# Weights for a gated feed-forward: nine transfers with the cast on GpSimd's queue instead of staged loads and casts on ScalarE, with the order of all steps made anew

## The chip, the cores and the metric

The kernel runs on one core of a Trainium2 chip. The metric is the device time of the core in microseconds. Before the change the median of four runs is 265.79 us (265.08 to 266.65).

## The reference

Two stages follow each other. The first is a linear recurrence with a complex decay per channel; its output is the `x` of the second, a feed-forward with a sigmoid gate. Shapes: batch 4, 8 heads, 768 positions, 48 channels per head; 3072 tokens of 384, inner width 1536. All inputs and the output are float32.

```python
mag = np.sqrt(a_re * a_re + a_im * a_im)
scale = np.minimum(mag, 0.999) / (mag + 1e-06)
a_re_n, a_im_n = (a_re * scale, a_im * scale)
for t in range(S):
    new_re = ar * S_re - ai * S_im
    new_im = ar * S_im + ai * S_re
    kv = np.einsum('bhd,bhe->bhde', k[:, :, t], v[:, :, t])
    S_re, S_im = (new_re + kv, new_im)
    y[:, :, t] = np.einsum('bhd,bhde->bhe', q[:, :, t], S_re)
...
gate = 1.0 / (1.0 + np.exp(-(x @ w_gate)))
val = x @ w_val
return (gate * val @ w_out).astype(np.float32)
```

## The kernel before

The positions are cut into six chunks of 128, which makes 24 slabs (a batch and a chunk; a slab is 128 positions by 384 channels). Slabs are taken in seven groups of 4, 4, 4, 4, 4, 2 and 2 (`SIZES`); a group is one chunk of two or four batches.

For each slab the decay is brought into logarithmic and angular form. `lr` and `la` load the real and imaginary part of `a` (L568), `sq` squares them on ScalarE, for slabs 4 to 8 on VectorE (L595, L598), `add` and `min` form and cap the squared magnitude, `lnm`, `lna` and `inv` are Ln, Ln and Exp on ScalarE over a whole group (L619 to L630), `r` divides the imaginary by the real part, and `atan` is the arctangent on ScalarE over a whole group (L714). `add`, `min`, `r` and `qke` run on VectorE for group 0 and on GpSimd from group 1 on. TensorE sums logarithms and angles along the positions by multiplying with triangular matrices (`cl` L645, `ct` L728 or L750). From `cl` come the growth factors `ee` (Exp, L652 and L654); from `ct`, after taking off whole turns (`r16` on VectorE, `nid` on TensorE L764) and `ab` (VectorE, L785), come sine and cosine, `cs` (L796 to L799). `cr` (ScalarE, L774) keeps the last angle of a chunk for the next one; from chunk 2 on `hop` (L741), a small accumulating DMA from GpSimd's queue, adds it.

`lk`, `lq` and `lv` load k, q and v (L568). `v16` (GpSimd, L700) turns v into float16, `qke` multiplies q and k by `ee`, and `ks` and `qs` by `cs` (VectorE, L809). Then comes attention within the chunk: transposes `tp` (TensorE) copied by `qkT` (VectorE), or a transposing DMA from slab 13 on (L830), scores `sc` (L866), masked by `mst` (VectorE), output `y` (L932, L934) together with the state carried on by `kv`, `P`, `u` and `x16`. `y16`, `xp` and `xt` put the result into transposed float16 form; `xt` of all slabs of a group is the moving operand of the feed-forward.

For each group and each of 12 blocks of 128 inner channels, `pg` and `pv` are three matmuls each with `wg16` and `wv16` (L971), `tanh` on ScalarE makes the gate (L981), and `p` on VectorE multiplies gate and value (L987). `po` multiplies with `wo16` (L1007, three parts of four blocks), `ot` copies out of PSUM and `st` stores.

The weights are kept in SBUF as float16 for the whole run. They arrive in nine parts of 768 KB of float32: `wg` and `wv` for three thirds of the inner width, `wo` for three groups of four blocks. Each part is loaded on SP's queue into a staging buffer (`lw`, L540) and cast from there by ScalarE (`wg`, `wv`, `wo`, L547). The staging buffers are those of `p`: tag `"p"`, two of them, each holding two parts (`t_stage`, L465). A block's matmul waits for the cast of its part: `pg` and `pv` of blocks 0 to 3, 4 to 7 and 8 to 11 need part 0, 1 and 2, and `po`'s parts 0, 1 and 2 need `wo` 0, 1 and 2.

The order is written out. Every step has a due time in the table `TIMES`; `Plan.order` sorts all steps by it, and each engine executes its own steps in that order, SP and GpSimd their DMAs among them. `SLOTS` lists which buffer each tile takes, and where table sets of ScalarE change, a table load is put in (L1035). `WARM` gives, for some steps, a number of dummy matmuls of a zero matrix that TensorE does just ahead of the step (L1041), 212 in all. The semaphores of SP's DMAs are eight; each DMA there waits for the one eight places earlier.

```python
t_p = kind("p", 2, [L, NFB, NT], F16)
t_stage = kind("p", 2, [L, 2, DFF], F32)
...
for _ in range(WARM.get(key, 0)):
    nc.tensor.matmul(warm_of(tiles[st[2][0]]), zero, zero, start=True,
                     stop=True)
st[0](tiles)
```

Of the kernel before, what the change touches and what calls it, by code (L numbers as in the profile page):

```python
# [9 lines left out]
FT = mybir.ActivationFunctionType  # L10
# [26 lines left out]
    "lw": [  # L37
        19.49, 20.04, 30.47, 40.31, 47.2, 47.61, 46.25, 73.886, 81.267],
    "wg": [
        24.732, 43.572, 53.59],  # L40
    "wv": [
        28.793, 45.685, 56.737],
    "wo": [
        52.038, 79.752, 85.177],
    "lr": [
        0.6, 1.01, 3.72, 5.64, 7.56, 10.44, 19.08, 14.28, 24.164, 37.02,
        37.98, 45.84, 63.086, 73.476, 67.716, 68.676, 92.809, 95.026, 97.906,
        95.986, 131.5, 133.365, 166.445, 167.265],
    "la": [
        2.76, 4.68, 6.6, 1.42, 8.52, 13.32, 21.96, 12.36, 32.97, 42.78, 32.01,  # L50
        38.94, 66.756, 70.596, 69.636, 65.796, 93.556, 93.966, 98.866, 99.826,
        132.955, 137.236, 169.565, 166.855],
    "sq": [
        6.25, 8.17, 10.09, 9.13, 12.01, 16.953, 29.367, 20.803, 42.465,
        50.194, 44.948, 50.931, 71.7, 79.015, 73.917, 74.654, 98.023, 100.439,
        105.897, 105.16, 146.848, 141.69, 174.014, 172.8],
    "add": [
        7.119, 9.039, 10.959, 9.999, 13.027, 17.97, 30.384, 21.82, 44.139,
        51.099, 47.431, 55.186, 72.902, 81.822, 75.617, 78.122, 98.928,
        101.957, 109.068, 112.251, 148.29, 150.03, 174.919, 177.613],  # L60
    "min": [
        10.465, 11.539, 19.034, 31.449, 54.283, 59.633, 83.264, 79.763,
        104.673, 116.121, 154.388, 178.678],
    "lna": [
        10.958, 34.367, 63.259, 83.639, 112.029, 159.027, 181.383],
    "lnm": [
        12.335, 32.99, 64.636, 86.554, 117.088, 158.29, 180.646],
    "inv": [
        13.712, 35.875, 68.63, 87.931, 114.146, 159.895, 186.735],
    "r": [  # L70
        16.087, 15.221, 37.42, 40.36, 73.856, 70.175, 90.609, 100.197,
        124.829, 119.361, 164.309, 187.64],
    "cl": [
        13.863, 17.228, 15.601, 18.161, 37.278, 38.144, 35.069, 39.237,
        79.005, 71.394, 66.186, 69.454, 88.548, 112.467, 99.081, 114.653,
        139.626, 135.097, 135.743, 129.837, 162.384, 180.788, 181.657, 184.024],
    "ee": [
        15.356, 20.061, 21.541, 20.801, 38.125, 38.991, 37.252, 40.084, 82.9,
        73.177, 72.437, 70.483, 89.395, 116.263, 113.406, 115.523, 140.473,
        139.564, 137.607, 138.347, 163.231, 182.12, 182.86, 185.995],  # L80
    "scr": [
        28.52, 21.41, 22.37, 30.88, 42.23, 57.44, 48.02, 41.27, 83.456,
        82.777, 82.087, 83.736, 106.956, 116.819, 117.379, 117.099, 146.14,
        145.3, 145.86, 145.58, 176.685, 190.661, 183.416, 188.831],
    "rbe": [
        57.99, 60.708, 90.82, 119.819, 149.384, 194.771, 197.005],
    "lk": [
        15.24, 9.48, 27.12, 11.4, 21, 29.1, 48.3, 52.98, 74.436, 64.836,
        81.677, 86.967, 100.786, 106.546, 105.586, 123.678, 118.069, 107.506,
        158.098, 136.09, 168.605, 171.775, 175.235, 181.208],  # L90
    "lq": [
        16.2, 17.16, 30.06, 18.12, 41.82, 36.06, 48.78, 57.03, 75.396, 72.516,
        82.367, 96.946, 101.746, 109.426, 108.466, 126.359, 133.775, 112.315,
        159.058, 138.46, 172.445, 190.251, 175.905, 189.111],
    "lv": [
        28.11, 31.16, 40.86, 39.9, 62.676, 71.556, 63.846, 56.07, 84.016,
        103.666, 122.761, 102.706, 111.535, 144.89, 85.648, 118.479, 156.968,
        104.626, 156.558, 117.659, 135.13, 146.42, 181.619, 188.421],
    "v16": [
        39.783, 42.121, 46.855, 43.39, 68.913, 77.059, 81.246, 63.163, 92.946,  # L100
        113.205, 126.59, 121.702, 117.024, 153.811, 92.37, 144.793, 180.823,
        110.823, 176.251, 132.347, 152.257, 166.285, 198.483, 214.257],
    "qke": [
        19.69, 23.984, 34.227, 21.687, 52.522, 45.094, 57.64, 60.536, 84.746,
        87.087, 88.848, 102.912, 106.442, 117.6, 132.924, 129.129, 145.949,
        140.486, 162.548, 143.032, 182.185, 195.134, 183.946, 193.373],
    "atan": [
        17.39, 42.195, 77.638, 108.405, 128.051, 188.766, 189.503],
    "ct": [
        19.7, 21.064, 23.315, 22.491, 43.722, 45.48, 51.057, 48.16, 90.342,  # L110
        83.489, 86.435, 91.96, 122.348, 115.95, 130.651, 127.476, 140.92,
        146.098, 165.596, 164.583, 194.132, 197.143, 197.956, 204.107],
    "r16": [
        22.553, 23.019, 24.85, 23.518, 45.882, 46.973, 52.55, 56.052, 91.189,
        86.013, 87.282, 99.842, 124.156, 117.252, 131.498, 128.52, 146.898,
        149.406, 166.443, 165.446, 194.979, 199.289, 201.811, 206.04],
    "nid": [
        23.153, 23.961, 25.45, 24.124, 46.996, 47.573, 53.15, 57.25, 91.798,
        90.988, 90.012, 102.317, 125.791, 119.412, 132.144, 129.507, 150.204,
        155.105, 169.642, 166.242, 195.995, 201.192, 203.297, 213.571],  # L120
    "cr": [
        27.266, 30.169, 31.326, 28.423, 49.037, 51.668, 68.26, 59.378, 92.586,
        93.433, 97.177, 102.68, 127.311, 127.681, 144.386, 131.028, 156.626,
        160.632, 170.32, 167.763],
    "cs": [
        23.575, 26.109, 30.54, 27.636, 49.407, 48.039, 58.591, 59.748, 94.28,
        91.429, 95.543, 103.527, 126.154, 119.776, 133.911, 129.871, 151.782,
        155.469, 171.166, 166.606, 196.359, 201.556, 203.661, 214.248],
    "ks": [
        25.316, 27.635, 35.691, 32.495, 55.006, 49.236, 60.355, 66.904,  # L130
        96.644, 92.718, 98.376, 106.137, 127.627, 121.248, 135.716, 136.582,
        154.275, 159.937, 172.965, 169.831, 198.423, 202.845, 207.249, 215.537],
    "qs": [
        26.182, 28.501, 37.157, 33.361, 56.518, 50.702, 63.908, 69.383, 97.51,
        94.278, 104.374, 109.857, 132.43, 122.58, 138.513, 139.379, 156.452,
        167.841, 177.88, 174.431, 199.755, 211.988, 209.18, 218.223],
    "ab": [
        30.233, 27.169, 48.77, 48.039, 57.872, 58.938, 92.161],
    "tp": [
        27.788, 31.585, 30.692, 29.501, 38.79, 41.199, 40.553, 41.646, 62.391,  # L140
        60.202, 61.296, 63.485, 74.229, 75.522, 74.675, 72.911, 106.813,
        111.37, 98.634, 102.479, 116.596, 107.91, 113.113, 118.966, 154.258,
        143.708],
    "qkT": [
# [127 lines left out]
        203.866, 211.451, 220.798],  # L272
    "xq": [
        126.769, 141.65, 140.4, 164.125, 173.985, 179.589, 185.921, 200.886,
        213.009, 210.201, 219.548],
}
SLOTS = {
    "a2": "0101010",
# [793 lines left out]
```

## Time and profile before

| what | value |
|---|---|
| median of four runs | 265.79 us |
| profiled execution, its own time | 265.76 us |
| its span, first to last instruction | 263.9 us |
| TensorE matmuls busy | 244.2 us (93%), 2128 instructions |
| weight loads into TensorE | 155.4 us (59%) |
| VectorE | 210.4 us (80%), 363 |
| ScalarE | 190.2 us (72%), 297 |
| GpSimd | 144.4 us (55%), 156 |
| SP's DMA queue (q1) | 41.28 MB in 174320 packets, 76.5% of 16 DMA engines |
| GpSimd's DMA queue (q0) | 0.03 MB in 512 packets, 0.2% |
| mean granted TensorE clock | 0.974 |

The span is the stretch from the first to the last instruction; the execution's own time has 1.8 us more around it. In the page, PE, ACT, DVE, POOL and SP are TensorE, ScalarE, VectorE, GpSimd and SyncE; L568 and the like are lines of the kernel. A slice row gives the busy tenths of 40 equal slices of the span. A table of windows gives, for each stretch, its length and then the busy time and the number of instructions (x) of TensorE's matmuls, its weight loads, VectorE, ScalarE and GpSimd, then the granted clock, the DMA engines' busy share and GB/s. The chain of waits is followed back from the last instruction (here, from the last in a window): each piece has its start, its length, and the engine or transfer that held the end up.

### The profile page before, as it was taken

Reading aid. Unit: us, or ns where it says so; the run is one execution under the profiler, and the core shown is the slowest. Engines: PE = TensorE matmul, PEld = TensorE weight load, DVE = VectorE, ACT = ScalarE, POOL = GpSimd, SP = SyncE. Lnnn points to the kernel's source line nnn. Section 1 sums busy time; section 2 is a strip of 40 time slices with the busy share of each in tenths; the row PEclk is TensorE's granted clock in tenths of the full one; section 3 lists DMA queues with packets and bytes.
Section 4 is the critical chain, followed back from the end, with each engine's and each line's share of the span. In section 5 each row is a group of like instructions: output and inputs, shape, how many; then the busy total and the mean of one; then the engine's idle time right before and its main releaser. Section 6 shows DMA issues by size and latency. Waiting matters only on the chain.

```text
span 263.9 us, 5745 instructions
## 1 busy us (share of the span) xinstructions
PE 244.2 (93%) x2128; PEld 155.4 (59%) x2128; DVE 210.4 (80%) x363; ACT 190.2 (72%) x297; POOL 144.4 (55%) x156
## 2 busy tenths in 40 slices
PE   8188399989899999999999999999999999999995
PEld 8145287454457664556775456754567554678784
DVE  2648997887999669898998869989957979796662
ACT  1899999689999899799669956778792674115140
POOL 3031207667499997789978399831989604011000
PEclk9959779999999999999999999999999999999999
DMA  7999999899999579995787987869986276540101
GB/s 150 211 192 292 224 222 191 207 362 138 123 195 248 161 152 163 218 190 122 95 190 161 199 192 73 160 132 210 216 156 114 31 149 79 112 132 30 45 18 62
DMA packets 174860, 41.68 MB, mean 158 GB/s; under 512 B 167768, under 2 KB 172528, under 8 KB 174832
## 3 DMA queue, kind: packets, MB, share of 16 engines
q1 hardware_dynamic: 174320, 41.28, 76.5%
q8 instruction: 17, 0.28, 0.4%
q0 software_dynamic: 512, 0.03, 0.2%
q14 instruction: 11, 0.09, 0.1%
HBM read 30.74 MB, written 4.76 MB: 135 GB/s over the span
## 4 chain that ended last, share of the span: by engine, by line
PE 61%; ACT 15%; SPq 8%; DMA 7%; DVE 4%; issue 4%; POOL 1%; ACTq 0%; DVEq 0%
PE o L1007 16%; PE v L971 14%; PE g L971 13%; SPq L568 7%; PE ct L750 4%; PE cl L645 4%; DMA stage<-in_moe_w_gate_dram 3%; PE sc L866 3%; ACT L1035 3%; DMA stage<-in_moe_w_val_dram 2%; ACT g L981 2%; PE y L934 2%; DMA a<-in_a_im_dram 1%; PE y L932 1%; ACT sq L598 1%
## 5 line engine op out<-in xcount | busy, mean ns | idle before, releaser
L981 ACT ACTIVATE g<-g 128x512 f16<-128x512 f32 (+1 forms) x84 | 43.3, 539 | 35.6 <-PE g L971 28.5
L987 DVE SCALAR_TENSOR_TENSOR p<-g,v 128x512 f16<-128x512 f16 (+1 forms) x84 | 49.3, 606 | 14.2 <-PE v L971 6.9
L971 PE MATMUL v<-xt,wv 128*128 128x512 f16 (+1 forms) x252 | 56.6, 348 | 0.9 <-ACT g L981 0.9
L971 PE MATMUL g<-xt,wg 128*128 128x512 f16 (+1 forms) x252 | 56.8, 348 | 0.0
L1007 PE MATMUL o<-wo,p 128*128 128x384 f16 (+1 forms) x300 | 54.6, 319 | 0.0
L707 POOL TENSOR_TENSOR qk<-qk,ee 128x768 f32<-128x768 f32 x20 | 39.7, 2055 | 8.5 <-ACT ee L654 4.6
L604 POOL TENSOR_TENSOR lm<-sq 128x384 f32<-128x384 f32 x20 | 21.9, 1097 | 39.8 <-DVE sq L595 24.2
L874 DVE TENSOR_TENSOR mst<-sc,msk_t 128x512 f16<-128x512 f32 x48 | 32.2, 685 | 5.8 <-PE sc L866 5.2
L971 PEld LDWEIGHTS <-wg 128*128 128x128 f16 x252 | 24.0, 98 | 20.9 <-issue 2.7
L971 PEld LDWEIGHTS <-wv 128*128 128x128 f16 x252 | 23.8, 98 | 20.1 <-issue 2.0
L1007 PEld LDWEIGHTS <-p 128*128 128x128 f16 x300 | 27.1, 97 | 13.8 <-issue 0.7
L1035 ACT ACT_TABLE_LOAD x23 | 29.5, 1283 | 0.4
L645 PE MATMUL cl<-lm,wl_t 128*128 128x384 f32 x48 | 22.6, 560 | 7.0 <-ACT lm L625 6.3
L809 DVE TENSOR_TENSOR kst<-qk,cs 128x768 f16<-128x768 f32 x24 | 25.1, 1047 | 1.5 <-issue 0.8
L809 DVE TENSOR_TENSOR qst<-qk,cs 128x768 f16<-128x768 f32 x24 | 24.7, 1032 | 0.0
L636 POOL TENSOR_TENSOR a<-a 128x768 f32<-128x768 f32 x10 | 19.0, 1902 | 7.6 <-ACT a L630 7.5
L854 DVE COPY qkT<-tp 128x1024 f16<-128x1024 f16 x26 | 17.5, 683 | 4.3 <-PE tp L848 4.3
L1041 PEld LDWEIGHTS <-zero 128*128 128x128 f16 x212 | 16.3, 114 | 6.4 <-issue 4.6
L598 ACT ACTIVATE sq<-a 128x768 f32<-128x768 f32 x19 | 15.7, 851 | 5.7 <-DMA a<-in_a_im_dram 5.6
L847 PE MATMUL tp<-idn_t,kst 128*128 128x128 f16 x104 | 15.4, 231 | 4.6 <-DVE cs L785 2.5
L796 ACT ACTIVATE cs<-ct 128x384 f32<-128x384 f32 x17 | 8.3, 490 | 15.5 <-PE ct L764 15.4
L700 POOL TENSOR_SCALAR v<-v 128x384 f16<-128x384 f32 x24 | 14.5, 604 | 5.3 <-DMA v<-in_v_dram 1.8
(76 smaller groups left out, 455.4 us busy)
## 6 DMA issues: line engine op xcount, KB each, us to landing
a<-in_a_re_dram SPq DMA_DIRECT2D x24, 192.0 KB
a<-in_a_im_dram SPq DMA_DIRECT2D x24, 192.0 KB
qk<-in_k_dram SPq DMA_DIRECT2D x24, 192.0 KB
qk<-in_q_dram SPq DMA_DIRECT2D x24, 192.0 KB
v<-in_v_dram SPq DMA_DIRECT2D x24, 192.0 KB
out_dram<-ot SPq DMA_DIRECT2D x23, 192.0 KB
stage<-in_moe_w_gate_dram SPq DMA_DIRECT2D x3, 768.0 KB
stage<-in_moe_w_val_dram SPq DMA_DIRECT2D x3, 768.0 KB
```

The source lines that it names most:

```text
L568: nc.sync.dma_start(heads(dst), src[b, :, c * L:(c + 1) * L].rearrange("h t d -> t h d"))
L604: eng(g).tensor_tensor(out=T[LM][:, s], in0=T[SQ][:, 0], in1=T[SQ][:, 1], op=ALU.add)
L636: eng(g).tensor_tensor(out=T[A][:, 1, i:j], in0=T[A][:, 1, i:j], in1=T[A][:, 0, i:j], op=ALU.mult)
L645: nc.tensor.matmul(T[CL][:, :HD], wl_t, T[LM][:, s], start=True, stop=True)
L707: eng(g).tensor_tensor(out=T[QK], in0=T[QK], in1=T[EE], op=ALU.mult)
L809: nc.vector.tensor_tensor(out=T[SL][i].rearrange("p h (r x) -> p h r x", r=2)[:, :, :, 0:D], in0=heads(T[QK][:, i]).unsqueeze(2) .broadcas ...
L874: nc.vector.tensor_tensor(out=T[MS], in0=T[SC], in1=msk_t.unsqueeze(1).broadcast_to([L, 4, L]), op=ALU.mult)
L971: nc.tensor.matmul(T[ACC][:, :nt], w[:, j, fb * 128:fb * 128 + 128], T[XT][:, j, :nt], start=(j == 0), stop=(j == 2))
L981: nc.scalar.activation(out=T[G16][:, :nt], in_=T[PG][:, :nt], func=FT.Tanh, scale=0.5)
L987: nc.vector.scalar_tensor_tensor(out=T[PT][:, fb, :nt], in0=T[G16][:, :nt], scalar=1.0, op0=ALU.add, in1=T[PV][:, :nt], op1=ALU.mult)
L1007: nc.tensor.matmul(T[PO][:, :wd], T[PT][:, fb, s * L:(s + 1) * L], wo16[:, fb, c0:c0 + wd], start=(fb == 0), stop=(fb == NFB - 1))
L1035: nc.scalar.preload_act_table_set(SETS[key[1]])
```

## The change

The nine parts of the weights no longer pass through staging buffers. Each is one DMA on GpSimd's queue that reads float32 from HBM and writes float16 straight into `wg16`, `wv16` or `wo16`. The steps `lw` on SP and the casts on ScalarE are gone, and so is the second use of the `p` buffers. The tables `TIMES`, `SLOTS` and `WARM` are all new: steps come in another order on every engine, tiles take other buffers, and the dummy matmuls are 150 instead of 212, put in other places. What each step computes is unchanged.

```diff
@@ tiles @@
     t_p = kind("p", 2, [L, NFB, NT], F16)
-    t_stage = kind("p", 2, [L, 2, DFF], F32)
@@ weights @@
-    def stage(n, i, key, dst, src):
-        ST = f"stage_{n}"
-        if not i:
-            t_stage(ST)
-
-        def e(T):
-            nc.sync.dma_start(
-                T[ST][:, i].rearrange("p (j f) -> p j f", j=dst.shape[1]), src)
-
-        load = add(("lw", 2 * n + i), e, after=[("lw", 2 * n)] if i else [],
-                   new=[] if i else [ST], use=[ST] if i else [])
-
-        def e(T):
-            nc.scalar.activation(
-                out=dst, in_=T[ST][:, i].rearrange("p (j f) -> p j f",
-                                                   j=dst.shape[1]),
-                func=FT.Copy)
-
-        return add(key, e, after=[load], use=[ST])
-
     gv_keys, ou_keys = [], []
-    for n, f in enumerate(range(0, DFF, 512)):
-        for i, (nm, dst, src) in enumerate((("wg", wg16, moe_w_gate),
-                                            ("wv", wv16, moe_w_val))):
-            gv_keys.append(stage(
-                n, i, (nm, n), dst[:, :, f:f + 512],
-                src[:, f:f + 512].rearrange("(j p) f -> p j f", p=128)))
-    for n, j in enumerate(range(0, NFB, 4)):
-        ou_keys.append(stage(
-            3 + n // 2, n % 2, ("wo", n), wo16[:, j:j + 4],
-            moe_w_out[j * 128:(j + 4) * 128].rearrange("(j p) f -> p j f",
-                                                       p=128)))
+    for i, f in enumerate(range(0, DFF, 512)):
+        for nm, dst, src in (("wg", wg16, moe_w_gate), ("wv", wv16, moe_w_val)):
+            def e(T, dst=dst, src=src, f=f):
+                nc.gpsimd.dma_start(
+                    dst[:, :, f:f + 512],
+                    src[:, f:f + 512].rearrange("(j p) f -> p j f", p=128))
+
+            gv_keys.append(add((nm, i), e))
+    for i, j in enumerate(range(0, NFB, 4)):
+        def e(T, j=j):
+            nc.gpsimd.dma_start(
+                wo16[:, j:j + 4],
+                moe_w_out[j * 128:(j + 4) * 128].rearrange(
+                    "(j p) f -> p j f", p=128))
+
+        ou_keys.append(add(("wo", i), e))
@@ dummy matmuls @@
 WARM = {
-    ('cl', 0): 78,
-    ('cl', 1): 3,
-    ('cl', 2): 4,
+    ('cl', 0): 41,
+    ('cl', 2): 8,
     ('cl', 3): 2,
-    ('ct', 0): 16,
-    ('ct', 1): 2,
-    ('ct', 3): 14,
-    ('sc', 0, 0): 15,
-    ('sc', 1, 0): 8,
-    ('sc', 1, 1): 8,
-    ('sc', 2, 1): 12,
-    ('sc', 3, 0): 9,
-    ('y', 3): 5,
-    ('pg', 0, 0): 8,
-    ('pg', 0, 10): 3,
-    ('cl', 6): 15,
-    ('ct', 4): 8,
-    ('cl', 10): 2,
+    ('ct', 0): 7,
+    ('ct', 2): 16,
+    ('y', 2): 11,
+    ('sc', 3, 1): 9,
+    ('pg', 0, 0): 11,
+    ('cl', 4): 15,
+    ('cl', 6): 30,
 }
```

Of the new order, the stretch in front of the first feed-forward block, as each engine has it (numbers are slabs, for `lnm`, `lna`, `inv`, `atan` groups, for weights parts):

```
ScalarE: cs0 cs1 cr0 cr1 cr3 cs3 cr2 cs2 lnm1 lna1 ee6 inv1 ee4 ee5 ee7 atan1 sq9 cs5 cr4 cr5 cs4 sq11 sq10 lna2 cs7 cr7 tanh
VectorE: ks0 qs0 sq6 ks1 r16.2 ab3 qs1 ab2 ks3 qke2 ... mst3 ks5 y16.3 xt0 qs5 y16.2 xt3 r16.7 ks4 xt2 xt1
GpSimd:  add4 add5 add7 v16.0 min4 wg0 add6 min6 r6 r4 wv0 v16.1 add8 add9 qke4 wg2 qke5 v16.3 wv2 v16.2 add10 wg1 min8 qke6 wv1 add11 v16.6 min10 qke7 add12 wo1 v16.4 arr1 r8 wo0 r10 ... wo2
```

In the order before, ScalarE has in this stretch the casts wg0 behind cs0, wv0 behind cr3, wg1 behind atan1, wv1 behind sq10, wo0 and wg2 behind cr5, and wv2 behind the first tanh; wo1 and wo2 come later, behind sq13 and lna3.

## The prediction

> **What bounds the kernel now.** I read the page's slices first, then the busy time by stages, then the chain of waits for the first 64 us, then the rows of the lines that the change touches. In the first fence come slices of 6.6 us, in the second stages with each engine's busy us and instruction count.
>
> ```profile
> PE   8188399989899999999999999999999999999995
> ACT  1899999689999899799669956778792674115140
> DMA  7999999899999579995787987869986276540101
> ```
>
> ```profile
> 0.00:60.00 60.00, 45.72 (x408) 31.89 (x408) 44.29 (x81) 49.04 (x63) 22.71 (x33) 0.89 0.97 228
> 60.00:70.00 10.00, 8.75 (x72) 4.83 (x70) 8.43 (x12) 9.89 (x15) 6.93 (x7) 1.00 0.92 111
> 70.00:80.00 10.00, 9.81 (x72) 5.41 (x71) 9.59 (x14) 9.90 (x16) 7.59 (x8) 1.00 0.95 186
> 80.00:100.00 20.00, 19.51 (x199) 12.63 (x198) 15.32 (x30) 19.22 (x24) 18.98 (x20) 1.00 0.78 178
> 100.00:120.00 20.00, 19.72 (x140) 10.70 (x139) 18.54 (x27) 18.21 (x31) 15.76 (x15) 1.00 1.10 197
> 120.00:240.00 120.00, 119.82 (x1042) 72.92 (x1040) 101.70 (x173) 77.61 (x136) 72.44 (x78) 1.00 0.73 139
> ```
>
> There are two regimes. From 70 us to 240 TensorE stands still for 0.19 + 0.49 + 0.28 + 0.18 = 1.14 us, so the end is set by how early the dense stretch of matmuls begins and by the few gaps after that. Before 60 us TensorE is the least loaded of the resources that matter: its 45.7 busy us contain nearly all of the dummy matmuls (17.9 us for the kernel), while ScalarE and the DMA engines (share 0.97) are full. The change can only pay before about 60 us and in the gaps just behind.
>
> The chain of waits (start, us, what) shows how the dense stretch begins:
>
> ```profile
> 33.66 4.02 SPq L568
> ...
> 43.09 6.39 DMA stage<-in_moe_w_val_dram
> ...
> 49.50 1.49 ACT wv L547
> ...
> 51.01 7.59 DMA stage<-in_moe_w_gate_dram
> ...
> 58.62 1.48 ACT wg L547
> ...
> 60.12 1.28 ACT L1035
> ...
> 61.41 0.60 ACT g L981
> ```
>
> The weights arrive late on SP's queue, ScalarE casts them in order, and the first tanh (L981, 61.41) stands behind the casts of 56.50 and 58.62. The timeline of TensorE has the first gate matmul at 59.17, with the blocks behind it broken by waits for that tanh (0.64 us at 63.9).
>
> ```profile
> L547 ACT ACTIVATE wg<-stage x3: 1467/1483/1483, 26.0 to 58.6; 128x1536 f16<-128x1536 f32 x3
> L547 ACT ACTIVATE wv<-stage x3: 1476/1484/1485, 30.6 to 61.9; 128x1536 f16<-128x1536 f32 x3
> L547 ACT ACTIVATE wo<-stage x3: 1467/1484/1484, 56.5 to 92.3; 128x1536 f16<-128x1536 f32 x3
> ...
>   DMA stage<-in_moe_w_val_dram: 1.0, 1
>   DMA stage<-in_moe_w_out_dram: 0.9, 2
>   DMA stage<-in_moe_w_gate_dram: 0.8, 2
> ```
>
> ```profile
> L741 POOL DMA_DIRECT2D a<-cr x16: 793/819/1282, 85.8 to 206.4; - x16
> ```
>
> The first of these two fences has min/median/max ns of the casts and how long ScalarE sat idle before them; the second is the only DMA that GpSimd issues in this trace.
>
> **What the Trainium skill says.** "DMA: Bandwidth & Descriptors", section "Anatomy of one DMA — SWDGE (gpsimd) path": a DMA from GpSimd has its descriptors written by GpSimd's own cores; many can be written "before the incremental cost shows up"; its fit is 2.0 us plus bytes at 436 GB/s, an estimate of 3.8 us for 786 KB. The hops agree as to the fixed part (1.9 to 4.8 us to landing); no large one is in the trace. The same page, "Queues, rings and completion order": each DMA engine takes turns between queues by packets. So a weight on GpSimd's queue should not wait behind SP's backlog; this trace has no two loaded queues to show it. "SBUF — State Buffer", "SBUF: two separate sides": a VectorE instruction in a two-port mode locks GpSimd out of writing descriptors, 620 ns becoming about 3100. "VectorE: DVE Perf Modes", "Mode 2×_2P": that mode needs its single source in SBUF. From 43 to 60 us VectorE's one-source work here reads PSUM (r16, ab, y16, qkT, xt, P) and the rest has two inputs, so I expect no such lock there; the hops among similar work (median 819 ns) agree.
>
> **The change, part by part.**
>
> *Casts.* 9 x 1.48 = 13.3 us leave ScalarE, seven of them (10.4 us) starting by 61.9, with three waits for weights of 2.7 us in all. They can't all be gained: VectorE is 44.3 busy of 60, and 9.28 + 9.38 of 20 between 20 and 40.
>
> *Path to the first gate matmul.* I walk the new order with durations of the trace; a start-to-start distance is used where the trace has it. Up to the first cs (24.50) ScalarE's steps are the same kinds in the same sequence. Then: cs, cs at 1.28 and three cr at 0.50 to 28.6; the third cs waits for VectorE's ab, which stands behind ks 0.86, qs 0.87, sq 0.87, ks 0.86, r16 0.47, ab 0.47 from 25.8, thus 30.2; cs 0.93, cr 0.50, cs 0.93, table 1.28 lead to Ln at 33.9 (before 35.32); Ln 1.39, Ln 1.49, ee 0.75, Exp 1.50 to 39.05. The two r on GpSimd (1.90, 1.82) end at 42.8, and group 1's arctangent starts at 42.9, against 44.92 before.
>
> *GpSimd's queue.* Behind the r stand, in this order: weight wv0, v16, add, add, qke, wg2, qke, v16 of slab 3, wv2, v16 of slab 2. That last one feeds y of slab 2 and so the first gate matmul. Three weight issues are on this path. Take q for one: nothing in the trace has 384 rows. Below, the hop's 0.82 + 0.07 gap = 0.89; above, the lock's 3.1. I take 1.0, since it writes more descriptors, but without a lock. Sum from 42.8: 3 x 1.0 + v16 3 x 0.58 + add 2 x 1.05 + qke 2 x 1.90 = 10.6, so v16 of slab 2 ends at 53.4. VectorE's queue from there: y16 0.48, xt 0.30, r16 0.47, ks 0.86, two xt 0.60, with y itself 0.35: 3.1, so the first gate matmul at 56.6. That is 2.6 before 59.17. The walk leaves out waits that I can't see (landings of q, k and v, pipeline gaps), so I book 1.6 of it: about 57.6.
>
> *DMA.* A weight at the 304 GB/s of the window 50 to 60 costs 2.6 us of all engines. Before, seven weights are issued by 51.5, and SP, which reuses eight semaphores, stood still for 4.02, 3.40 and 3.71 us in its issues (33.7, 53.2, 56.7). Afterwards six stand before the first tanhs and wo follows in GpSimd's queue later; nine issues of 0.35 to 1.04 us leave SP, so the a, q, k and v loads behind them go sooner. I book no separate gain; it is what lets the walk hold. A weight lands, by the trace's 6.4 and 7.6 us, in time: wv2 issued by 52.8 is there by 60.4, and its first use comes about four blocks of 0.65 us after the first, roughly 60.5, so a wait of up to 0.5 is possible; wg1 (issued about 55) and wv1 (about 59) are needed nine and more blocks in.
>
> *Behind the first matmul.* TensorE's gaps are 1.25 us from 60 to 70 and the 1.14 above. In that time casts at 61.9, 86.2 and 92.3 (4.4 us) leave a ScalarE that is 99% busy to 80 and 96% to 100. GpSimd takes four issues more there, being 18.98 busy of 20 from 80 to 100, but these come before 80. I book 0.8 of 2.4.
>
> *Dummies, buffers, order.* Dummies fall from 212 to 150; they fill idle time, so nothing is gained. They hold the granted clock at 1.00 from 36 us; should a window of some 6.8 us drop to half, as at 29.4 here, up to 3 us are lost. Freed p buffers and the order after 100 us: nothing, TensorE is full there and its work is the same.
>
> Sum: 1.6 + 0.8 = 2.4. The profiled execution took 265.76, its span being 263.9 and 1.8 lying around it, and stands 0.03 below the median of 265.79: 263.4.
>
> **Rivals.**
>
> *GpSimd's issues are dear (slower).* A weight's issue holds GpSimd for q, and three stand ahead of slab 2's v16. For it: 384 rows on either side against the hop's 16, and the skill's lock. Against it: the hops, and VectorE's sources in PSUM. Each 0.1 costs 0.3 us; it decides from q = 1.0 + 2.4/3 = 1.8, where the gain is gone, and makes the kernel measurably slower from 2.25. At q = 2.6 the time is 263.4 + 3 x 1.6 = 268.2.
>
> *VectorE and the DMA engines take ScalarE's place (no change).* VectorE has under 5 us of slack between 20 and 60 and the DMA share is 0.97; the transfer with a cast may hold the engines longer. Then the first gate matmul comes at about 58.8 and the gaps remain: 265.4. Against it: the walk went through VectorE's queue and still gained.
>
> *All of it is gained (much faster).* The walk's whole 2.6 and 2.0 of the gaps: 261.2. For it: ScalarE is on the chain in nearly every step from 8.5 to 26 and again from 49.5; against: no walk of this kind is without waits.
>
> *The change does what it says* without a rival: the plain loads and casts are gone from SP's and ScalarE's order, and nine DMAs stand in GpSimd's.
>
> **How the numbers follow.** Forecast 0.42 (its own range 262.3 to 264.4), all gained 0.15, no change 0.21, dear issues 0.17, another cause of loss (clock, late weight) 0.05. About 0.5%, 1.3 us, is what a measurement can tell from no change, so faster is below 264.5 and slower above 267.1. Faster 0.57, same 0.22, slower 0.21. Leaving a tenth on each side: 261.2 to 267.8.
>
> **What would show it.** Right: first gate matmul between 56.5 and 58.2, arctangent of group 1 near 43, no wait for a weight over 0.5 us, GpSimd's DMA rows near 1.0 us, TensorE's gaps from 60 to 120 below 2 us. Wrong: DMA rows of GpSimd above 1.8 us, slab 2's v16 later than 55, a gate or value matmul released by a weight's landing, or a clock below 1.00 after 40 us.

## The result, and the profile after

The median after is 264.8 us (264.25 to 266.14, 41 runs), before 265.75 us (264.47 to 267.29, 62 runs); the ratio is 0.9965, 95% interval 0.9955 to 0.9976. So 0.95 us (0.35%) are gained of the 2.4 us forecast, within the 0.5% that the prediction took for what a measurement can tell from no change. A second measurement, on another occasion, gave 0.9938 (0.9919 to 0.9957): after took 264.76 us again, before 266.56. So the size of the gain depends on how before runs on that occasion. The forecast of 263.4 us is missed; the time lies inside the range of 261.2 to 267.8 us. A few runs lie more than 1.5% above the fastest of their kernel; ratios leave them out, medians hold them. The span is 263.1 us (263.9 before), the mean granted clock 0.974 in both.

The slices of after, each 6.6 us:

```profile
PE   6086778999999999999999999999999999999995
ACT  3699599299999578999459648758974373214240
DMA  7999999999699959975699969869964455551011
```

The busy us and instruction counts by stages, in the columns used for before:

```profile
0.00:60.00 60.00, 42.52 (x351) 27.81 (x352) 45.49 (x83) 44.60 (x62) 29.12 (x38) 0.89 1.02 183
60.00:70.00 10.00, 10.00 (x75) 5.80 (x74) 8.84 (x12) 9.73 (x15) 6.78 (x8) 1.00 0.90 128
70.00:80.00 10.00, 9.99 (x71) 5.31 (x69) 8.79 (x14) 9.95 (x19) 9.79 (x11) 1.00 1.22 210
80.00:100.00 20.00, 19.49 (x204) 12.60 (x203) 16.63 (x30) 14.36 (x18) 19.15 (x22) 1.00 0.87 164
100.00:120.00 20.00, 19.52 (x128) 10.55 (x127) 18.16 (x26) 19.44 (x33) 16.07 (x16) 1.00 0.89 159
120.00:240.00 120.00, 119.34 (x1075) 72.56 (x1074) 103.39 (x176) 73.92 (x130) 69.47 (x75) 1.00 0.72 137
```

From 60 to 80 us TensorE's gaps are closed: 1.25 and 0.18 us more busy than before. Behind that TensorE stands still a little more than in before: 0.02, 0.20 and 0.48 us in the last three stages.

The weights' rows on GpSimd (busy us, mean ns of one):

```profile
L526 POOL DMA_DIRECT2D wg<-in_moe_w_gate_dram x3 | 2.7, 895 | 0.1
L526 POOL DMA_DIRECT2D wv<-in_moe_w_val_dram x3 | 2.5, 840 | 0.1
L533 POOL DMA_DIRECT2D wo<-in_moe_w_out_dram x3 | 2.5, 820 | 0.0
```

An issue takes 0.80 to 1.03 us, close to the 1.0 assumed. The chain of waits of after, from group 1's arctangent to the first gate matmul (start, us, what; some pieces are left out), has no weight in it:

```profile
43.51 1.49 ACT a L687
...
48.92 0.34 DVE r L730
...
52.49 0.56 DVE cs L758
53.05 0.60 DVE mst L847
53.64 0.87 DVE kst L782
...
57.30 0.86 DVE kst L782
58.17 0.54 DVE xt L931 x2
58.71 0.04 issue
58.75 0.81 PE g L944 x3
```

VectorE's queue leads to the first gate matmul at 58.75, only 0.42 us ahead of the 59.17 of before.

Neither that matmul nor the busy share says how far a kernel has come, so I count work: each matmul but the dummies, weighted with the spacing at which back-to-back ones of its form start in these traces (0.216 us for 512 columns, 0.163 for 384, 0.056 for 128, 0.026 for 48, other widths in proportion, twice as much in float32). Both kernels have 217.6 us of it. The table says at what time of each trace so much of it is left:

```
work left, us    200    195    190    180    150    120     80     60   none
before         51.81  60.71  66.66  77.99 109.44 140.11 180.22 200.47 260.60
after          51.57  59.93  65.02  75.40 106.30 137.82 178.36 199.64 259.72
after-before   -0.24  -0.78  -1.64  -2.59  -3.14  -2.29  -1.86  -0.83  -0.88
```

The new order gains 3.1 us up to 106 us and gives back 2.3, in two steps: 0.85 between 150 and 120 us left, 1.03 between 80 and 60. I call a matmul's start late when it comes 0.12 us or more later than the spacing allows; the time given is that of the matmul ahead of it. TensorE's late starts behind 75 us are, in before, 0.65, 0.44 and 0.34 us at 88.5, 102.9 and 122.1, together 1.4; in after 0.67, 0.17, 0.23, 0.57, 0.17, 0.26, 0.15, 0.69 and 0.18 at 92.4, 103.4, 113.4, 114.1, 129.2, 143.0, 188.5, 190.2 and 195.9, together 3.1. Those at 113 to 129 us and at 188 to 196 us fall into the two steps. The timeline of after shows the largest three with their releasers:

```profile
93.11 0.18 PE L907 MATMUL y<-v,mst 128*128 128x48 f16 x1 [0.51 <-POOL v L673]
...
114.86 0.81 PE L944 MATMUL v<-xt,wv 128*128 128x512 f16 x3 [0.41 <-ACT g L954]
...
190.87 0.81 PE L980 MATMUL o<-wo,p 128*128 128x384 f16 x4 [0.53 <-ACT g L954]
```

The largest of before is of the same kind as the first of these, a y that waits for its v16 on GpSimd (slab 6 there, slab 7 here), so the new order did not bring it:

```profile
89.19 0.18 PE L934 MATMUL y<-v,mst 128*128 128x48 f16 x1 [0.49 <-POOL v L700]
```

The second trace of after has the same late starts at the same places, each within 0.01 us of the first, but for the 0.15 at 188.5. Of before there is one trace only. The old order with the new path of the weights (e1, below) has late starts of 2.3 us by the same count, so part of the difference between 1.4 and 3.1 may belong to the occasion or to the path and not to the order.

### The profile page after: what moved, and what is told of

It reads as the page before. It is cut to its first block, busy times and chain, and to the rows that moved or that the text cites. A ratio compares the mean times of both kernels' runs of the same rounds, so it can differ in the third digit from the quotient of the medians.

```text
span 263.1 us, 5644 instructions
## 1 busy us (share of the span) xinstructions
PE 240.8 (92%) x2066; PEld 150.7 (57%) x2066; DVE 212.3 (81%) x363; ACT 178.5 (68%) x288; POOL 150.4 (57%) x165
## 3 DMA queue, kind: packets, MB, share of 16 engines
q0 software_dynamic: 4496, 3.57, 9.7%
## 4 chain that ended last, share of the span: by engine, by line
PE 57%; DVE 11%; ACT 9%; SPq 7%; POOL 6%; issue 4%; DMA 4%; DVEq 0%; POOLq 0%; ACTq 0%
PE o L980 15%; PE v L944 13%; PE g L944 13%; SPq L541 7%; PE ct L723 4%; PE sc L839 3%; DVE p L960 2%; DVE kst L782 2%; PE cl L618 2%; ACT L1008 2%; ACT a L687 2%; DVE qst L782 2%; DMA qk<-in_q_dram 1%; POOL a L609 1%; DMA qk<-in_k_dram 1%
## 5 line engine op out<-in xcount | busy, mean ns | idle before, releaser
L944 PE MATMUL v<-xt,wv 128*128 128x512 f16 (+1 forms) x252 | 57.3, 348 | 0.5 <-ACT g L954 0.4
L577 POOL TENSOR_TENSOR lm<-sq 128x384 f32<-128x384 f32 x20 | 22.5, 1142 | 31.4 <-DVE sq L568 18.9
L680 POOL TENSOR_TENSOR qk<-qk,ee 128x768 f32<-128x768 f32 x20 | 38.1, 1912 | 2.7 <-ACT ee L627 1.2
L782 DVE TENSOR_TENSOR qst<-qk,cs 128x768 f16<-128x768 f32 x24 | 26.7, 1119 | 0.0
L782 DVE TENSOR_TENSOR kst<-qk,cs 128x768 f16<-128x768 f32 x24 | 24.4, 1026 | 1.4 <-ACT cs L772 0.9
L609 POOL TENSOR_TENSOR a<-a 128x768 f32<-128x768 f32 x10 | 18.1, 1814 | 9.2 <-DMA qk<-in_q_dram 7.8
L861 POOL TENSOR_TENSOR state<-state,arr 128x384 f32<-128x384 f32 x16 | 13.9, 867 | 10.9 <-DVE state L889 10.6
L625 ACT ACTIVATE ee<-cl 128x384 f32<-128x384 f32 x24 | 12.0, 501 | 9.0 <-PE cl L618 6.9
L723 PE MATMUL ct<-a,wt_t 128*128 128x384 f32 x40 | 17.5, 524 | 0.5 <-ACT a L687 0.3
L839 PEld LDWEIGHTS <-qkT 128*128 128x128 f16 x192 | 13.4, 97 | 7.3 <-issue 2.7
```

What stands on the lines that cost most here:

```text
L577: eng(g).tensor_tensor(out=T[LM][:, s], in0=T[SQ][:, 0], in1=T[SQ][:, 1], op=ALU.add)
L680: eng(g).tensor_tensor(out=T[QK], in0=T[QK], in1=T[EE], op=ALU.mult)
L723: nc.tensor.matmul(T[CT][:, :HD], wt_t, T[A][:, 1, s], start=True, stop=False, skip_group_check=True)
L782: nc.vector.tensor_tensor(out=T[SL][i].rearrange("p h (r x) -> p h r x", r=2)[:, :, :, 0:D], in0=heads(T[QK][:, i]).unsqueeze(2) .broadcas ...
L839: nc.tensor.matmul(sc[:, i], kt, qt, start=True, stop=True)
L944: nc.tensor.matmul(T[ACC][:, :nt], w[:, j, fb * 128:fb * 128 + 128], T[XT][:, j, :nt], start=(j == 0), stop=(j == 2))
```

## The experiments

Ratios are against the kernel before, measured beside each experiment on the same chip. In e1 to e4 that one took 267.95 us where it had taken 265.75, so their expected times, which rest on 265.75, are read as ratios. In the cuts of code, `MOVED` gives steps new due times, by the number of the slab, group or part, and `...` stands for lines left out. "Point 180" is the time at which 180 us of matmul work are left (before 77.99, after 75.40), "rest" what it takes from there to the last matmul (before 182.6, after 184.3).

### The path alone, the order alone

One kernel has before's order with the new path, one after's order with the old path.

```diff
-    "lw": [19.49, 20.04, 30.47, 40.31, 47.2, 47.61, 46.25, 73.886, 81.267],
-    "wg": [24.732, 43.572, 53.59],
+    "wg": [19.49, 30.47, 47.2],
...
```

> The order of before, with only the path of the weights changed: each of the nine transfers goes on GpSimd's queue with the cast in it, at the due time that its plain load had on SP; loads to staging buffers and casts on ScalarE are gone. Theory 'the transfer is what helps' : the first tanh no longer waits for the casts of 56.5 and 58.6 us, so the first gate matmul comes before 58.5 us and the time is 264.8 us or less, as much as the whole change gave (0.95 us). Theory 'the new order is what helps, the transfer alone is worth nothing': VectorE and the loads set the pace as they did, first gate matmul at 59.0 to 59.5 us, time 265.3 to 266.2 us. If GpSimd's issues cost it more than 1.0 us each, r or v16 come later and the time goes above 266.5 us.

Measured (e1): 267.87 us, ratio 1.0012 (0.9991 to 1.0034); first gate matmul 59.45, point 180 at 78.28, rest 183.4. ScalarE's timeline shows where the room went:

```profile
52.26 0.49 ACT L776 ACTIVATE cs<-ct 128x384 f32<-128x384 f32 x1 [4.84 <-DVE cs L764]
...
60.29 0.60 ACT L960 ACTIVATE g<-g 128x512 f16<-128x512 f32 x1 [2.43 <-PE g L950]
```

ScalarE idles 4.8 us for VectorE and 2.4 for TensorE. The path alone gains nothing that can be measured.

```diff
+    "lw": [19.49, 20.04, 30.47, 40.31, 47.2, 47.61, 46.25, 66.0, 75.5],
-    "wg": [22.939, 53.604, 46.761],
+    "wg": [24.732, 43.572, 53.59],
...
```

> The order of after, with staged loads on SP and casts on ScalarE put back at about the places that they had in before (two wo loads and casts some us earlier, since po needs them earlier). Theory 'the casts and their loads are the cost': 13.3 us come back on ScalarE, seven casts of them before the first tanhs, so the first gate matmul is 2 us or more later than the 58.8 us of after and the time is 266.5 to 269 us. Theory 'the order alone makes the difference': time within 0.5 us of after, 264.3 to 265.3 us.

Measured (e2): 278.9 us, ratio 1.038 (1.031 to 1.045), beyond both ranges; first gate matmul 65.40, first tanh 72.82, point 180 at 86.9. With the casts put back at these places the new order loses 3.8%. The size depends on the places, which nobody has tuned, so it isn't shown that no order with the casts could gain. Of the two parts as they were tried, neither gains alone.

### Making the first gate matmul earlier

```diff
+MOVED = {"ks": {4: 55.03, 5: 55.0}, "qs": {5: 55.01}, "r16": {7: 57.3},
+         "ct": {6: 55.4, 7: 56.7}, "sq": {10: 58.26, 11: 58.25},
+         "lna": {2: 62.4}, "add": {10: 58.3}, "wv": {1: 53.7},
...
+WARM.update({('y', 2): 0, ('pg', 0, 0): 4})
```

> After, with the stretch in front of the first gate matmul put in another order: on VectorE four products of group 1 (ks, qs, ks and r16 of slab 7) stand behind the four xt, on TensorE the angle sums of slabs 6 and 7 behind the first gate matmuls, on ScalarE two squares and the Ln of group 2 with its two table loads behind the first tanhs, fewer dummy matmuls there. The first gate matmul should come at 55.3 to 56.5 us in place of 58.75. Theory 'the end follows the first gate matmul': TensorE is full behind it, so 2.3 to 3.4 us are gained, time 261.4 to 262.5 us. Theory 'later steps of the other groups bind TensorE as well': what was moved comes back as waits of TensorE between 60 and 110 us, and the time is 264 to 265.5 us.

Measured (e3): 270.3 us, ratio 1.0102 (1.0064 to 1.0141). The matmul came at 56.43, 2.3 us earlier, and the kernel was slower, beyond both theories: point 180 at 81.5. Its timeline of TensorE:

```profile
56.43 1.44 PE L962 MATMUL g<-xt,wg 128*128 128x512 f16 x3 [0.49 <-DVE xt L949]
...
74.26 2.20 PE L636 MATMUL cl<-lm,wl_t 128*128 128x384 f32 x6 [1.86 <-ACT lm L616]
```

The work put behind that matmul still has to be done, and group 2's logarithms, put back with it, made TensorE wait at 74. To see whether those alone do it:

```diff
+MOVED = {"sq": {10: 58.26, 11: 58.25}, "lna": {2: 62.4}, "add": {10: 58.3}}
...
```

> After, with only ScalarE's work for group 2 moved: its two squares (1.56 us) and its Ln with the two table loads (4.05 us) stand behind the first two tanhs instead of before them, and one add on GpSimd with them. The first tanh can come when the first gate matmul is done, about 1.2 us earlier than 60.97. Theory 'what the casts left on ScalarE is worth something because group 2's logarithms fill it': TensorE waits for lm of group 2 behind 68 us, as it did for 2.0 us when more was moved, and the ratio to before goes up to 1.001 to 1.007. Theory 'the first tanh is what counts': ratio 0.990 to 0.994.

Measured (e8): 268.64 us, ratio 1.0069 (1.0042 to 1.0096), point 180 at 79.1. These alone cost much of it, in the range of the first theory: the waits of TensorE up to 73 us are 1.9 for tanh and 1.3 for lm. The first tanh came at 62.2, not earlier. The other way round, these logarithms early in before's order with the new path:

```diff
+MOVED = {"lna": {2: 56.0}, "lnm": {2: 62.5}, "inv": {2: 64.67},
+         "r": {4: 70.4, 5: 67.7}, "atan": {2: 76.35}}
...
```

> The order of before with only the path of the weights changed (ratio 1.0012), and in addition group 2's logarithms where after has them: Ln before the first tanhs, in the 2.4 us that ScalarE now idles there, and its other Ln, Exp and r steps some us earlier. Theory 'the room that the casts left on ScalarE is only worth something when group 2's logarithms go into it': the arctangent of group 2 comes 2 to 4 us before the 84.5 us that it had, and the ratio falls to 0.993 to 0.998. Theory 'the gain of the new order is spread over many steps': ratio 0.9995 to 1.003.

Measured (e11): 266.65 us, ratio 1.0013 (0.9994 to 1.0032). Ln came at 58.0 in place of 69.3 in e1, and the last r on GpSimd ended at 79.7 in place of 82.1. Yet group 2's arctangent came at 84.6, as in e1 (84.5): on ScalarE an `ee`, squares, two tanhs and a table load still stand between. So early logarithms are part of the gain (e8) and, moved by themselves, bring nothing, since the steps behind them keep their places. That it takes the order of several engines at once fits this; it was not tried.

### Issues and bytes of the weights

```diff
+MOVED = {"wg": {1: 52.1}, "wv": {1: 52.15}, "wo": {0: 57.4, 1: 53.6, 2: 64.7}}
...
```

> After, with five of the nine weight transfers issued earlier, in places where GpSimd stands idle or in each other's former places: wg and wv of the middle third at the idle stretch behind v16 of slab 2 (53.3 us), the three of wo by 69 us in place of 69.9, 73.3 and 78.5. That takes 2.5 us of issues out of GpSimd's stretch from 69 to 100 us, in which it is 97% busy. Theory 'GpSimd's queue, with the issues in it, is what binds there': hops, v16 of slab 7 and the qke behind them come up to 2.5 us sooner, the 0.67 us wait of y at 92.4 us goes, time 0.5 to 1.3 us below after, ratio to before 0.991 to 0.9945. Theory 'the issues are hidden': the same ratio as after within 0.0015.

Measured (e10): 266.25 us, ratio 0.9997 (0.9971 to 1.0024), beside 0.9938 for after: 1.5 us slower, neither theory. The waits between 69 and 73 us (total, times, longest):

```profile
PE tp L827 <- ACT ee L634: 1.6, 1, 1.6
ACT sq L578 <- DMA a<-in_a_im_dram: 1.4, 1, 1.4
```

The wait of y for v16 of slab 7 stayed (0.67). What moved was a load of a on SP's queue: with more weights under way its issue, at 57.2, held SP for 5.03 us (0.95 in after), its square began 1.4 us later than in after (69.39 against 68.00) and held up Exp behind it on ScalarE, and TensorE waited 1.6 us. Behind that nothing changed: rest 184.4. Then the bytes and the issues were taken away:

```diff
-                    dst[:, :, f:f + 512],
-                    src[:, f:f + 512].rearrange("(j p) f -> p j f", p=128))
+                    dst[:, :, f:f + 16],
+                    src[:, f:f + 16].rearrange("(j p) f -> p j f", p=128))
...
```

> After, with the nine weight transfers cut to 16 columns of each part, one thirty-second (wg, wv) or one twenty-fourth (wo) of the bytes, with as many rows; the rest of the weights is a constant written at the start, so that the output is another one. The issues on GpSimd stay. Theory 'the transfers take DMA time from the loads': six of them, of some 2.7 us of all engines each, lie in the stretch before 62 us in which the DMA share is 1.02, so loads come up to 10 us earlier there and the time falls by 2 to 6 us, ratio to before 0.972 to 0.988. Theory 'the transfers are hidden': within 0.2% of after, ratio 0.992 to 0.998.

Measured (e13): 264.84 us, ratio 0.9927 (0.9900 to 0.9953), point 180 at 75.9. The constant is written by three instructions of 2.0 us on GpSimd, done by 8.7 us, ahead of its first work on the inputs. Its later point 180 (75.4 in after) has another reason than the weights: ScalarE's first Ln already starts 0.5 us later, at 11.70, ahead of the first weight.

```diff
-            st[0](tiles)
+            if not (key[0] in ("wg", "wv", "wo")):
+                st[0](tiles)
```

> As the one before, with the nine transfers left out altogether, so that GpSimd has no weight issues (nine of 0.80 to 1.03 us). Theory 'the issues stand on the path', as the prediction had it for three of them in front of v16 of slab 2: v16 of slab 2 ends 2.4 us sooner, and the time is 0.8 to 2.4 us below the kernel with few bytes. Theory 'GpSimd's idle stretches hide them': within 0.3 us of it.

Measured (e14): 265.27 us, ratio 0.9943 (0.9920 to 0.9965), first gate matmul 59.13, point 180 at 75.8. That is 0.4 us above the kernel with few bytes, so outside the 0.3 of the second theory, but away from the first. The stage before the gate with no transfers, then with them (after, second trace):

```profile
40.00:60.00 20.00, 17.43 (x166) 10.34 (x166) 17.46 (x32) 14.04 (x21) 14.61 (x12) 1.00 0.64 126
```

```profile
40.00:60.00 20.00, 17.93 (x170) 10.53 (x168) 17.32 (x32) 14.20 (x21) 17.02 (x16) 1.00 1.05 182
```

GpSimd has 2.4 us less of work and the DMA share falls from 1.05 to 0.64. Yet the first gate matmul comes no sooner. Its timeline, GpSimd's v16 of slabs 3 and 2 and then TensorE:

```profile
50.29 1.10 POOL L675 TENSOR_SCALAR v<-v 128x384 f16<-128x384 f32 x2
...
52.37 0.91 PE L706 MATMUL ct<-cr,sel_t 32*128 32x384 f32 x2
53.21 0.63 PE L909 MATMUL y<-v,mst 128*128 128x48 f16 x8
...
53.84 0.78 PE L1016 MATMUL y<-zero 128*128 128x128 f16 x11
54.46 0.36 PE L909 MATMUL y<-v,mst 128*128 128x48 f16 x8
```

v16 of slab 2 ends at 51.4, 1.9 us sooner than in after, and the y that it feeds starts at 54.46 (54.59 in after), since on TensorE angle sums, the y of slab 3 and eleven dummy matmuls stand in front of it. In both kernels what was taken away brought nothing: where they stand in after, the weights cost nothing that can be measured.

### The waits behind 75 us

```diff
+MOVED = {"sq": {19: 108.5}, "v16": {7: 85.5}, "lna": {6: 186.9},
+         "inv": {6: 187.0}, "r": {11: 188.5}, "atan": {6: 195.0},
+         "hop": {14: 197.3, 15: 197.4}, "ct": {22: 203.5}}
...
```

> After, with the causes of three waits of TensorE behind 75 us moved: v16 of slab 7 ahead of a qke on GpSimd (y waited 0.67 us for it at 92.4), one square behind a tanh on ScalarE (0.57 us at 114.1), and Ln and Exp of the last group joined to its other Ln behind the tanhs (0.69 us at 190.2; two table loads of 1.28 us become one pair less). Theory 'what the new order loses behind 75 us are these waits': they add up to 1.9 us, and 1.2 to 1.9 us are gained, time 262.9 to 263.6 us. Theory 'TensorE is only the place where another engine's lateness shows': the waits turn up again at the next step and the time stays at 264.4 to 265.2 us.

Measured (e4): 267.09 us, ratio 0.9969 (0.9948 to 0.9989), so nothing gained on after; rest 186.3. Two waits for others, in the waits of 92 to 98 and of 205 to 211 us:

```profile
PE xp L937 <- ACT ee L639: 1.1, 1, 1.1
...
PE g L956 <- ACT g L966: 0.7, 1, 0.7
```

v16 went ahead of a qke on GpSimd, that of an Exp, and that held xp up by 1.1 us; the joined Ln put a table load in front of other tanhs. So in this try the waits turned up elsewhere. Next, load was taken off instead, one engine at a time: ScalarE's bursts, VectorE's qs, GpSimd's qke.

```diff
+LEFT_OUT = {("atan", 3), ("lna", 6), ("inv", 6)}
...
```

> After, with two bursts on ScalarE left out, so that part of the computation is not done: the arctangent of group 3 (1.49 us and its table load) at 110 us, and Ln and Exp of group 6 at 186 us (1.68 us and two table loads). TensorE waits 0.23 + 0.57 us behind the first and 0.15 + 0.69 us behind the second. Theory 'what the new order loses behind 100 us are TensorE's waits for tanh behind such bursts, one for one': 1.2 to 1.7 us less than after, ratio to before 0.990 to 0.992. Theory 'TensorE catches up elsewhere': within 0.5 us of after, ratio 0.9945 to 0.998.

Measured (e12): 265.15 us, ratio 0.9957 (0.9940 to 0.9974), rest 184.9. The wait at 114 us is still 0.6.

```diff
+            if not (key[0] == "qs" and key[1] >= 12):
```

> After, with the product qs left out for slabs 12 to 23 (12 instructions of about 1 us on VectorE, all behind 100 us), so that q of these slabs is stale and the output is another one. Theory 'TensorE's waits behind 100 us are at bottom waits for VectorE': of the 2.3 us of them 1 to 2 go, ratio to before 0.987 to 0.9925. Theory 'TensorE's own queue and other engines set them': within 0.3 us of after, ratio 0.993 to 0.998.

Measured (e15): 265.31 us, ratio 0.9950 (0.9932 to 0.9968), rest 184.9; waits as in after, and one more of 0.5 us at 187.

```diff
+            if not (key[0] == "qke" and key[1] >= 12):
```

> After, with the product qke left out for slabs 12 to 23 (12 instructions of 1.8 to 2.5 us on GpSimd, all behind 100 us), so that q and k of these slabs lack their growth factor and the output is another one. Theory 'the waits behind 100 us are at bottom waits for GpSimd' (16.1 of 20 us busy from 100 to 120): 1 to 2 us go, ratio 0.987 to 0.9925. Theory 'GpSimd has room there': within 0.3 us of after, ratio 0.993 to 0.998.

Measured (e16): 264.58 us, ratio 0.9916 (0.9885 to 0.9947), rest 184.1. The ratio reaches into the first theory's range, but the waits are those of after but for 0.17 us at 129, and the last matmul is 0.14 us earlier than in after's second trace: the second theory. In the waits between 112 and 116.5 us the releaser of TensorE is VectorE's p without the bursts, and without qs ScalarE's tanh, as in after:

```profile
PE v L945 <- DVE p L961: 0.4, 1, 0.4
```

```profile
PE v L944 <- ACT g L954: 0.4, 1, 0.4
```

So both were left out together.

> After, with both left out: ScalarE's bursts (arctangent of group 3, Ln and Exp of group 6, with their table loads) and VectorE's product qs for slabs 12 to 23. Theory 'ScalarE and VectorE hold TensorE together, so that each alone gains nothing': the waits at 113 to 114 us (0.8 us) go, and part of those at 188 to 196, 0.8 to 1.8 us less than after, ratio to before 0.988 to 0.992. Theory 'it is neither of them': waits and time as in after, ratio 0.9935 to 0.9975.

Measured (e17): 265.56 us, ratio 0.9984 (0.9968 to 0.9999), just above the second range, rest 185.1; the wait at 114 is 0.63. So that wait is set neither by these bursts of ScalarE nor by qs on VectorE, nor by both. The releasers, tanh or p, are the two steps that give an accumulator of the gate or value matmuls back to TensorE, which has four of them. That the wait is the way round through these four, in the order in which TensorE takes its blocks, fits these runs; it was not tried by itself, with more accumulators or with the blocks in another order. What causes the late starts behind 100 us stays open.

Can the early lead be joined to the old end? Three kernels out of two orders; the row of the arctangents shows which is which.

```diff
-        17.39, 41.764, 76.35, 105.833, 131.576, 183.842, 183.105],
+        17.39, 41.764, 76.35, 105.833, 128.051, 188.766, 189.503],
```

> One kernel out of two orders, weights by GpSimd: every step due before 108 us in after stands as in after, all others follow in the order of before. By the count of matmul work after is 3.1 us ahead of before at 104 us and 0.9 at the end. Theory 'the new order wins in its first part and loses 2 us in its second': the lead is kept, time some 2 us below after, 262.5 to 263.4 us where before is 265.75, a ratio to before of 0.988 to 0.991. Theory 'the lead cannot be kept, since loads or another engine bind the second part in any order': ratio 0.995 to 0.998, as after.

Measured (e5): ratio 1.0083 (1.0053 to 1.0113). The late starts of after are there up to 113 us; then the seam has five more, of 0.7, 1.0, 1.8, 0.3 and 1.1 us up to 125. One more of 0.5 us comes at 173. The last 60 us of work take 60.1 us, as in both kernels.

> The same with the cut at 135 us of due time (about 142 us in the trace): it keeps the waits that after has at 113 to 129 us (some 1.0 us) and leaves out those at 143 to 196 (some 1.3 us). Theory 'the second part of the new order loses': ratio to before of 0.991 to 0.9935, between after (0.9965) and the cut at 108. Theory 'the lead cannot be kept': 0.995 to 0.998.

Measured (e6): ratio 1.0117 (1.0082 to 1.0151); a seam of 1.3, 0.7, 0.3 and 2.0 us at 142 to 150, and 1.6 us at 175.

```diff
-        17.39, 41.764, 76.35, 105.833, 131.576, 183.842, 183.105],
+        17.39, 42.195, 77.638, 105.833, 131.576, 183.842, 183.105],
```

> The other way round, weights by GpSimd: every step due before 102 us in before stands as in the kernel with only the path of the weights changed (ratio 1.0012), all others follow in the order of after. Theory 'the second part of the new order loses 2 us': ratio 1.006 to 1.010. Theory 'the second part is as good as the old one': ratio 0.999 to 1.003.

Measured (e7): ratio 1.0171 (1.0130 to 1.0212); a late start of 1.2 us already at 87, where po waits 1.0 us for a transfer of wo, and 3.4 us of late starts from 110 to 135. All three missed both theories: the seam costs more than what was to be measured. By the due times at 108 us the new order has done steps that the old one has not, the arctangent of group 3 among them, and has still to make transposes of slabs 8 to 10 that the old one has made; these then come all at once. Whether the lead could be kept stays open.

### The control and the dummies

> After unchanged, as the measure for the three kernels beside it: ratio to before 0.9955 to 0.9976 as measured at first, and the same waits of TensorE behind 75 us (0.67, 0.23, 0.57, 0.17, 0.26, 0.69 us in the first trace) at the same places to within 0.1 us each.

Measured (e9): ratio 0.9938 (0.9919 to 0.9957), just below the expected range, though the time is the same as at first; point 180 at 75.42, rest 184.2, late starts as said above.

```diff
+WARM = {}
```

> After without any dummy matmul (150 of them in after). Theory 'they only keep the clock up': the granted clock of TensorE falls below 0.9 in more windows before 60 us, and matmuls on the path there take longer, 0.5 to 3 us more, ratio to before 0.998 to 1.008. Theory 'they cost nothing and bring nothing': within 0.3 us of after, 0.9935 to 0.9975.

Measured (e18): 265.51 us, ratio 0.9976 (0.9956 to 0.9996), just above the second range. The first two stages without dummies, then with them (after, second trace):

```profile
0.00:20.00 20.00, 4.77 (x8) 2.28 (x9) 9.86 (x27) 13.12 (x13) 5.38 (x17) 1.00 1.00 195
20.00:40.00 20.00, 12.12 (x52) 6.63 (x51) 17.89 (x24) 16.98 (x29) 6.28 (x6) 0.66 0.99 169
```

```profile
0.00:20.00 20.00, 9.87 (x58) 7.20 (x59) 9.87 (x27) 13.03 (x13) 5.28 (x17) 0.74 0.97 192
20.00:40.00 20.00, 14.46 (x129) 10.25 (x127) 18.21 (x24) 17.34 (x30) 6.71 (x7) 0.91 1.01 173
```

The granted clock is 1.00 and then 0.66 without dummies, 0.74 and then 0.91 with them. So between these two traces the clock differs in where it is low and not in sum. A third trace, with the same dummies (e17), has 1.00 and 0.91, so this also varies from one execution to the next. Point 180 comes 0.4 us later, and by the last matmul that is made up (259.71). Their worth is between nothing and 0.4%; the medians, from different occasions, differ by 0.7 us.

## Why the prediction was right and wrong

- **The walk.** Ln at 33.9 (measured 34.58), r's end 42.8 (43.2), arctangent 42.9 (43.51), v16 of slab 2 ending at 53.4 (53.25): right. The last piece, "VectorE's queue from there: ... 3.1", took 5.5 us. From y16 of slab 2 on it took 2.73, as the walk has it (2.71). But this y16 began at 56.02, where the walk has it at 53.75: y itself came only at 54.59 on TensorE, and on VectorE, which ScalarE had held until 52.49, the ks of slab 5, y16 of slab 3, an xt and the qs of slab 5 stand in front, which the walk left out. Of the 1.6 us booked there, 0.42 came.
- **"Behind the first matmul."** Of the 2.4 us of gaps, 0.8 were booked. From 60 to 80 us 1.43 went.
- **The two together.** At point 180 after is 2.6 us ahead, where the sum said 2.4. So the first part has the forecast's size, but by luck: one term was too large, the other too small, and some 0.7 us lie in neither. The first gate matmul was the wrong mark: it says when one kind of work begins, and e3 had it 2.3 us sooner and was slower.
- **The step that failed:** "Freed p buffers and the order after 100 us: nothing, TensorE is full there and its work is the same." The work is the same and the fullness is not. Of a lead of 3.1 us at 106 us, 2.3 are lost by the end where the sum has nothing. Counted from point 180, after takes 184.3 us for what takes before 182.6; these 1.7 us are the difference of the late starts, 3.1 against 1.4, and they turn 2.6 into 0.9. An order that is all new could change any place where a step comes just in time. The prediction took busy shares for the answer, and these hide late starts of a few tenths of a us. What makes these starts late stays open: taking load off ScalarE, VectorE or GpSimd left most of them in place (e12, e15, e16, e17), and the one trace of before leaves open how much of the 1.7 us another trace of it would show.
- **The cause of the gain.** The prediction has most of the gain from the casts leaving ScalarE's order; e1, with the old order and no casts, shows nothing. The gain came with path and order changed together. The new order with the casts put back loses 3.8% (e2), at places that were not tuned.
- **GpSimd's issues**, three of 1.0 us on the path: the price was about right (0.80 to 1.03), and they did not set the first gate matmul. v16 of slab 2 came when the walk said, and 1.9 us sooner without them, but y didn't wait for it: TensorE's queue did (e14).
- **Transfers**: "I book no separate gain; it is what lets the walk hold." The first half is right (e13, e14); the second isn't borne out, since without transfers no feed-forward matmul came sooner. The Trainium skill, "DMA: Bandwidth & Descriptors", section "Queues, rings and completion order", has each DMA engine take turns between queues. A weight landed in 5.7 to 6.6 us in the median beside a loaded SP queue, against the 6.4 and 7.6 us of two weights on SP's queue in the chain of before. That agrees with turns and doesn't single them out. In e10 SP's queue is held up when more weights are under way.
- **Dummies**: between nothing and 0.4%, below the "up to 3 us". They "hold the granted clock at 1.00 from 36 us", but without them it is 1.00 from 40 us on too, and the mean of the trace is the same as with them (0.974, e18).
- **Readings.** The lines give five waits for weights, not three (2.7 us is right). 53.4 and 3.1 make 56.5, not 56.6. And of SP's three long issues that of 3.40 us at 53.2 was for a buffer that ks on VectorE gave back late (3.3 us), not for the eight semaphores.
- **Rivals.** The issues' price of 1.8 us was not reached. The rival of no change (265.4) came nearest, and not for its reason: VectorE did hold the first gate matmul (58.75, it said 58.8), but the gaps did not remain. Every sign set for the forecast but the gate's time came out right; none of them looked behind 120 us.

## What to carry to other kernels

Where one engine is full from some point on, compare two kernels by how much of its work is left at the same time, not by when one instruction begins; and add up its late starts to the very end: here starts late by 0.15 to 0.7 us took back most of what had been gained. A transfer or an issue that is hidden where it stands is not hidden everywhere: all nine weights cost nothing that could be measured in after, and five of them, issued 4 to 13 us earlier, cost 1.5 us. Of this tuned order no part could be moved or joined by itself: each such try was no faster than after, and most waits that were taken away turned up at a later step (e4, e12).

## What the runs showed that I had not expected

- Removing 9 of 9 weight transfers (3.57 MB as written, 9.7% of the 16 engines' span) took the DMA share between 40 and 60 us from 1.05 to 0.64 and v16 of slab 2 forward by 1.9 us, and no feed-forward matmul came sooner.
- Two traces of after, on different occasions, give late starts equal to 0.01 us, but for one. Runs of after scatter less: beside the second measurement 22 of after lie within 264.49 to 266.49, 64 of before within 264.63 to 268.01. The kernel with the old order and the new path scatters like before (266.74 to 269.89). But so do kernels that differ little from after (e10 265.39 to 268.31, e18 264.75 to 267.68), so that the new order is the reason isn't shown.
- With 150 dummy matmuls the clock was 0.74 in the first 20 us and 0.91 in the next 20, without them 1.00 and 0.66, with the same mean of 0.974 in both traces. The time changed by no more than 0.4%.
